# Linear attention with a gated MLP: the query sums as unsplit fp32 products in two column halves of the array, and GpSimd in program order around them

## The chip, the cores and the metric

The kernel runs on one core of one Trainium2 chip. TensorE (PE in the profile) multiplies matrices, with its weight loads recorded separately (PEld); VectorE (DVE), ScalarE (ACT) and GpSimd (POOL) do elementwise work; SyncE (SP) and GpSimd issue DMA transfers. A fp32r operand is a 32-bit number that TensorE reads in one pass at reduced precision; a number split into two fp32r parts, high and low, keeps nearly all of fp32's digits. The metric is the device time in microseconds of one execution, the median of several runs.

## The reference

One input x of 2048 tokens by 576 features goes through two layers, and a gate per token mixes them. The attention layer has 32 heads of 18 features, and each head's feature map phi has 36 (two softmaxes).

```python
pq = einsum("bhsd,hdf->bhsf", q, w_phi)
phi_q = concatenate([softmax(pq), softmax(-pq)])      # the same for phi_k
kv = einsum("bhsf,bhsd->bhfd", phi_k, v)
z = einsum("bhsf->bhf", phi_k)
num = einsum("bhqf,bhfd->bhqd", phi_q, kv)
den = einsum("bhqf,bhf->bhq", phi_q, z)[..., None] + 1e-6
a = (num / den) @ wo                                  # heads side by side
h = (x @ W_gate) * (x @ W_gate > 0) * (x @ W_up)
b = h @ W_down                                        # 4608 hidden features
return g * a + (1 - g) * b                            # g = sigmoid(x . gate_w)
```

## The kernel before, in words

**Stages.** The 2048 tokens are 16 tiles of 128, or four blocks of 512, worked through in the order 3, 0, 1, 2 (`BLOCKS`); "block 0" to "block 3" below count in that order. From 0 to 262 us the kernel makes projections, softmaxes, and the key sums kv and z over all tokens. From 262 to 300 us it makes the query sums (num and den) of blocks 0 and 1. From there to 365 us it divides, multiplies by wo (`project_out`, tiles pw, lines 738 to 759) and makes the sums of blocks 2 and 3 between. From 365 to 400 us the last output projection overlaps the start of the MLP, and from 400 us the MLP runs alone.

**Query sums.** Heads lie in groups: three heads are 54 output columns and 108 rows of phi (`QK`); eleven such groups hold 32 heads (`NQ`; the last has two). `sums` (L537) makes the sums of two groups, that is six heads, in one PSUM tile, as 108 columns of num and six of den (`QM` = 114). Each group takes three fp32r products of 512 columns: weights high by queries high, high by low, low by high. Six pairs of groups are taken in the order 4, 5, 3, 2, 1, 0 (`ORDER`). The weights kvm are a block-diagonal arrangement of kv and z, split into kvh (L527) and kvl (L531). The queries of block 0 are turned in place from PSUM (`turn`, ptr) into their parts phh and phl (L150, L151). Those of the other blocks go to memory (eT) and come back tile by tile as er (`fetch`, L425), and ACT (L435) and DVE (L439) split them.

**What follows a sum.** `sums_out` (L546) copies the PSUM tile to R, or to the separate tile og for pairs 4 and 5 (L552, ACT). SP sends the den rows to a tile dn (L554). GpSimd issues the fills (L556, L559, L560): they move num rows of og into free rows of R, so that five full tiles of 128 rows come out. `invert` (L695) takes the reciprocal of dn, multiplies it by the gate and splits it into rdh and rdl (L706, L708). `divide` (L711) spreads them over the rows with a product (pd) and multiplies R by it (L717); the result is split into oh and ol for the product with wo. `rows_out` (L762) copies the finished rows and stores them to att, by GpSimd for three of the blocks.

**What sets the order.** A scheduler orders the instructions of each engine by their dependences and by tile buffers, apart from those named in `in_order` (L53): there the engine keeps the order of the program. Before, that holds for TensorE only. Each engine then carries out its own list strictly in order, and so does each queue of DMA issues. A tile whose buffer is still read by an earlier user makes its writer wait. `scale` (L210) multiplies the softmax numerators e by the reciprocals of their sums; the last ones, on GpSimd, stand in this stretch.

**The hand-over.** `load_w` (L830) loads raw MLP weights (wr, 768 KB each) that ACT and DVE split into wb and ws (`unit`, L887). On SP they stand where the scheduler finds their buffer free.

Of the kernel before, what the change touches and what calls it, by code (L numbers as in the profile page):

```python
# [35 lines left out]
QM = G + 2 * QH  # L36
# [46 lines left out]
def gated_mix_kernel(  # L83
# [281 lines left out]
    def turn(t, b, ps=None):  # L365
# [52 lines left out]
    def operands(tb):  # L418
        PH[tb] = [[ph.tile([QK, len(n), TB], F32R, name=f"ph{a}{n.start}") for a in "hl"] for n in QN]

    ER = {}
# [5 lines left out]
    def part(tb, i, p):  # L427
        if tb not in PH:
            operands(tb)
        return *(a[:, :, i * P:(i + 1) * P] for a in PH[tb][p]), ER[4 * tb + i][:, QN[p].start:QN[p].stop]  # L430

    def prepare_high(tb, i, p):

        h, l, r = part(tb, i, p)
        nc.scalar.activation(h, r, AF.Copy)  # L435

    def prepare_low(tb, i, p):
        h, l, r = part(tb, i, p)
        tt(out=l, in0=r, in1=h.bitcast(F32), op=SUB)  # L439
# [16 lines left out]
    for t in range(2, NT - 2):  # L456
# [10 lines left out]
        if t == 12:  # L467
# [6 lines left out]
            ph = RS.enter_context(tc.tile_pool(name="ph", bufs=1, **R_))  # L474
# [35 lines left out]
    def kv_blocks(q):  # L510

        n, ps = min(4, NQ - 4 * q), PKV[q]
        for p in range(2):
# [7 lines left out]
            else:  # L521
                tt(out=kvm[:, gs_, p * QG:(p + 1) * QG], in0=ps[:, p:n:2, 1 + p * QG:1 + (p + 1) * QG],
                   in1=mask[:, None, :].to_broadcast([QK, ng, QG]), op=MULT)
            nc.vector.scalar_tensor_tensor(
                out=kvm[:, gs_, G + 3 * p:G + 3 * p + 3], in0=ps[:, p:n:2, 0:1].to_broadcast([QK, ng, 3]),
                scalar=eps, in1=hm[:, None, :].to_broadcast([QK, ng, 3]), op0=ADD, op1=MULT)
        nc.scalar.activation(kvh[:, 4 * q:4 * q + n, :QM], kvm[:, 4 * q:4 * q + n], AF.Copy)  # L527

    def kv_low(q):
        n = min(4, NQ - 4 * q)  # L530
        tt(out=kvl[:, 4 * q:4 * q + n, :QM], in0=kvm[:, 4 * q:4 * q + n],  # L531
           in1=kvh[:, 4 * q:4 * q + n, :QM].bitcast(F32), op=SUB)

# [3 lines left out]
    def sums(tb, i, ps):  # L537

        PS[tb, i] = ps = ps[:QM]
        parts, pairs = PH[BLOCKS[tb]], []  # L540
        for g in range(2 * i, min(2 * i + 2, NQ)):
            (h, l), o = parts[g // 4], g % 4
            pairs += [(kvh[:, g, :QM], h[:, o]), (kvh[:, g, :QM], l[:, o]), (kvl[:, g, :QM], h[:, o])]
        accumulate(ps, pairs)

    def sums_out(tb, i):  # L546
# [4 lines left out]
        og = OG[i] = R[:QM, i] if i < 4 else rb.tile([P, TB], F32, name="og")[:QM]  # L551
        nc.scalar.activation(og, PS.pop((tb, i)), AF.Copy)  # L552
        d0, dl = (G, HG) if i < NJ - 1 else (G + 1, 2)
        nc.sync.dma_start(dn[4 * HG * i:4 * (HG * i + dl)], og[d0:d0 + dl])  # L554
        if i < 4:
            nc.gpsimd.dma_start(R[G:, i], OG[4][20 * i:20 * i + 20])  # L556
# [34 lines left out]
    with in_order(tc, nc, nc.tensor):  # L591
# [10 lines left out]
        er = RS.enter_context(tc.tile_pool(name="er", bufs=4, **R_))  # L602
# [3 lines left out]
        kvm = kb.tile([QK, NQ * QM + 26], F32, name="kvm")[:, :NQ * QM].rearrange("p (g c) -> p g c", g=NQ)  # L606
        kvh = kb.tile([QK, NQ, P], F32R, name="kvh")
        kvl = kb.tile([QK, NQ, P], F32R, name="kvl")
# [4 lines left out]
        for i in range(4):  # L613
            fetch(i)
# [13 lines left out]
        kv_low(2)  # L628
# [3 lines left out]
        kv_low(1)  # L632
        turn(t, 0)
        kv_low(0)
# [4 lines left out]
        for n, i in enumerate(ORDER):  # L639
# [22 lines left out]
        for i in range(4):  # L662
            prepare_high(b1, i, 0)
            prepare_low(b1, i, 0)
# [230 lines left out]
    def prepare_tile(n, i):  # L895
        tb = BLOCKS[n]
        for p in (2, 1, 0):
            prepare_high(tb, i, p)
            prepare_low(tb, i, p)

# [20 lines left out]
    with in_order(tc, nc, nc.tensor):  # L921
# [14 lines left out]
        for i in range(4):  # L936
            fetch(4 * BLOCKS[2] + i)
        inv = invert(1)
        for k in range(5):
# [8 lines left out]
            if k < 3:  # L948
                prepare_tile(2, k)
            if k >= 3:  # L950
                divide(1, k - 3)
                project_out(0, k - 2, (1,))
                if k == 3:
                    prepare_tile(2, 3)
# [19 lines left out]
        for i in range(4):  # L974
            fetch(4 * BLOCKS[3] + i)
# [8 lines left out]
        for k in range(5):  # L984
            project_out(1, k)
            if k < 4:
                prepare_tile(3, k)
# [584 lines left out]
def _layout(A_x, A_wqkv, A_w_phi, A_wo, B_W_gate, B_W_up, B_W_down, gate_w):  # L1572
# [17 lines left out]
    wo_rows = [r for k in range(4) for r in (*range(G * k, G * k + G), *range(4 * G + 20 * k, 4 * G + 20 * k + 20))]  # L1590
    wo_rows += [*range(512, D)] * 2
# [40 lines left out]
```

## Time and profile before

| what | us |
|---|---|
| median of 3 runs | 1642.44 (1641.4 to 1642.8) |
| profiled execution: span | 1636.5 |
| TensorE busy in it | 1604.4 (98%) |
| TensorE busy, 262 to 300 us | 30.74 of 38, mean clock 0.91 |
| TensorE busy, 300 to 365 us | 65.00 of 65 |
| TensorE busy, 365 to 400 us | 30.05 of 35 |

The runs' times lie some 6 us above the span, which counts from the first to the last recorded instruction. A group row reads: line, engine, operation, output <- input, shapes, count | busy us, mean ns | idle time of the engine just before, and what ended it. A timeline row reads: start, duration, engine, line, operation, output <- input, and in brackets the idle time before it. Records of one matmul overlap those of the next, so their spacing, not their length, tells what one costs.

### The profile page before, as it was taken

Reading aid. Unit: us, or ns where it says so; the run is one execution under the profiler, and the core shown is the slowest. Engines: PE = TensorE matmul, PEld = TensorE weight load, DVE = VectorE, ACT = ScalarE, POOL = GpSimd, SP = SyncE. Lnnn points to the kernel's source line nnn. Section 1 sums busy time; section 2 is a strip of 40 time slices with the busy share of each in tenths; the row PEclk is TensorE's granted clock in tenths of the full one; section 3 lists DMA queues with packets and bytes.
Section 4 is the critical chain, followed back from the end, with each engine's and each line's share of the span. In section 5 each row is a group of like instructions: output and inputs, shape, how many; then the busy total and the mean of one; then the engine's idle time right before and its main releaser. Section 6 shows DMA issues by size and latency. Waiting matters only on the chain.

```text
span 1636.5 us, 20150 instructions
## 1 busy us (share of the span) xinstructions
PE 1604.4 (98%) x7732; PEld 1348.2 (82%) x7732; DVE 1232.1 (75%) x1908; ACT 581.4 (36%) x962; POOL 182.3 (11%) x266
## 2 busy tenths in 40 slices
PE   9999998998999999999999999999999999999998
PEld 8898997787788888888888887778888888888887
DVE  4988777758777777877777777667777677777777
ACT  4344335645333333332333334222322323223231
POOL 0128212220000000000000002111111111111110
PEclk9999999999999999999999999999999999999999
DMA  8243115565865656555645533553444434344442
GB/s 266 94 145 153 58 46 189 188 203 205 305 234 196 232 217 234 213 209 213 223 189 190 193 143 129 190 205 140 160 150 145 180 127 183 128 172 154 148 163 73
DMA packets 64860, 285.80 MB, mean 175 GB/s; under 512 B 7290, under 2 KB 16890, under 8 KB 55804
## 3 DMA queue, kind: packets, MB, share of 16 engines
q1 hardware_dynamic: 61932, 278.22, 46.9%
q0 software_dynamic: 2256, 5.25, 1.0%
q8 instruction: 61, 1.00, 0.2%
q10 hardware_dynamic: 576, 1.05, 0.2%
q14 instruction: 35, 0.29, 0.1%
HBM read 172.99 MB, written 109.54 MB: 173 GB/s over the span
## 4 chain that ended last, share of the span: by engine, by line
PE 87%; DVE 4%; DMA 4%; issue 2%; ACT 2%; POOL 1%; SPq 0%; ACTq 0%; DVEq 0%; POOLq 0%
PE cx L1132 26%; PE ca L1132 13%; PE pd L1172 12%; PE pd L1195 10%; PE cy L1132 7%; PE pq L177 3%; PE pv L177 2%; PE pk L177 2%; PE pm L1172 2%; PE pw L759 2%; PE pm L1195 2%; PE kv L411 2%; DMA wdr<-wd 1%; PE ptr L371 1%; PE pv L239 1%
## 5 line engine op out<-in xcount | busy, mean ns | idle before, releaser
L1239 ACT ACTIVATE hh<-g 128x512 fp32r<-128x512 f32 x195 | 120.0, 624 | 454.5 <-DVE g L1289 285.2
L1210 DVE TENSOR_TENSOR ac<-pd,ac 128x512 f32<-128x512 f32 x238 | 164.0, 689 | 146.4 <-PE pd L1195 146.3
L1132 PE MATMUL cx<-xo,ws 128*128 128x512 f32 x1008 | 252.7, 390 | 4.9 <-ACT g L1293 4.9
L1132 PE MATMUL ca<-xo,ws 128*128 128x512 f32 x1008 | 252.0, 389 | 0.6 <-DMA ws<-wsd 0.6
L1132 PE MATMUL cx<-xo,wb 128*128 128x512 f32 x1008 | 249.4, 390 | 3.0 <-DMA wb<-wbd 1.7
L1132 PEld LDWEIGHTS cx<-xo,ws 128*128 128x128 f32 x1008 | 189.1, 188 | 45.4 <-ACT g L1293 6.2
L1132 PEld LDWEIGHTS cx<-xo,wb 128*128 128x128 f32 x1008 | 188.0, 188 | 44.7 <-DVE u L1414 2.2
L1132 PEld LDWEIGHTS ca<-xo,ws 128*128 128x128 f32 x1008 | 189.1, 188 | 40.3 <-issue 1.0
L1172 PE MATMUL pd<-hh,wd 128*128 128x512 f32 x576 | 200.7, 389 | 0.0
L1195 PE MATMUL pd<-hh,wd 128*128 128x512 f32 x476 | 185.2, 389 | 0.0
L1178 DVE TENSOR_TENSOR ac<-pd,ac 128x512 f32<-128x512 f32 x144 | 99.0, 688 | 105.8 <-PE pd L1172 102.3
L1244 DVE TENSOR_TENSOR hl<-g,hh 128x512 fp32r<-128x512 f32 x195 | 136.1, 698 | 1.9 <-ACT hh L1239 0.2
L1293 ACT ACTIVATE g<-cx 128x512 f32<-128x512 f32 x144 | 85.0, 590 | 127.4 <-PE cx L1132 127.3
L1132 PE MATMUL cy<-xo,wb 128*128 128x512 f32 x504 | 127.2, 392 | 0.0
L1172 PEld LDWEIGHTS pd<-hh,wd 128*128 128x128 f32 x576 | 108.1, 188 | 22.5
L1095 ACT ACTIVATE wd<-wdr 128x384 fp32r<-128x384 f32 (+1 forms) x106 | 62.3, 606 | 155.7 <-DMA wdr<-wd 155.7
L1172 PE MATMUL pd<-hl,wd 128*128 128x512 f32 x288 | 112.1, 389 | 1.0 <-ACT xo L821 1.0
L1132 PEld LDWEIGHTS cy<-xo,wb 128*128 128x128 f32 x504 | 95.6, 190 | 20.1
L1195 PEld LDWEIGHTS pd<-hh,wd 128*128 128x128 f32 x476 | 89.4, 188 | 18.6
L1195 PE MATMUL pd<-hl,wd 128*128 128x512 f32 x238 | 92.6, 389 | 0.0
L805 POOL TENSOR_TENSOR xo<-xr,xo 32x512 fp32r<-32x512 f32 x5 | 8.2, 1651 | 634.6 <-DVE xo L805 627.3
L1098 DVE TENSOR_TENSOR wd<-wdr,wd 128x384 fp32r<-128x384 f32 (+1 forms) x106 | 69.7, 672 | 6.4 <-ACT wd L1095 6.4
(241 smaller groups left out, 2732.1 us busy)
## 6 DMA issues: line engine op xcount, KB each, us to landing
wsd<-ws SPq DMA_DIRECT2D x34, 1280.0 KB
ws<-wsd SPq DMA_DIRECT2D x34, 1280.0 KB
wbd<-wb SPq DMA_DIRECT2D x34, 960.0 KB
wb<-wbd SPq DMA_DIRECT2D x34, 960.0 KB
wr<-wgu SPq DMA_DIRECT2D x36, 768.0 KB
wdr<-wd SPq DMA_DIRECT2D x36, 576.0 KB
eT<-et SPq DMA_DIRECT2D x12, 594.0 KB
er<-eT SPq DMA_DIRECT2D x12, 594.0 KB
```

The source lines that it names most:

```text
L177: nc.tensor.matmul(ps, w, m, start=i == 0, stop=i == len(pairs) - 1)
L411: nc.tensor.matmul(kv[j // 2][:vn + 1, j % 2, :gn], v[:, j * GS:j * GS + vn + 1], flat(e)[:, c0:c0 + gn], start=False, stop=t == NT - 1, s ...
L1095: nc.scalar.activation(o[:, 0], a, AF.Copy)
L1098: tt(out=o[:, 1], in0=a, in1=o[:, 0].bitcast(F32), op=SUB)
L1132: nc.tensor.matmul(ps, w, v, start=first and m == 0, stop=m == len(pairs) - 1, skip_group_check=True)
L1172: nc.tensor.matmul(ps, w, v, start=k == 0 and (i < 2 or first), stop=k == len(mms) - 1 and (i < 2 or last), skip_group_check=True)
L1178: tt(out=a, in0=ps, in1=a, op=ADD)
L1195: mm = lambda ps, w, v, a, z: nc.tensor.matmul(ps, w, v, start=a, stop=z, skip_group_check=True)
L1210: tt(out=a, in0=ps, in1=a, op=ADD)
L1239: nc.scalar.activation(h, src, AF.Copy)
L1244: tt(out=l, in0=src, in1=h.bitcast(F32), op=SUB)
L1293: nc.scalar.activation(a, ps, AF.Copy)
```

## The change

Each group of three heads becomes one fp32 product of unsplit weights (kvm, 64 columns: 54 of num, three of den, the rest zero) and unsplit queries. The even group of a pair goes to the PSUM partitions 0 to 63 and the odd one to 64 to 127, which are the two halves of the array's columns. The splits of kvm and of the queries go, with the parts phh, phl, kvh, kvl and the tiles er; the queries of blocks 1 to 3 are loaded straight into place, with two buffers, and with an earlier place in the program. The copies take 128 rows, each pair's den rows are two DMAs instead of one, and a block's fills are 14 instead of 8, with fewer rows each. The rows of wo and spread are permuted on the host to fit. GpSimd joins TensorE in program order in the stretch that ends with block 1's turning.

```diff
-QM = G + 2 * QH
+QM = 64
...
         if t >= FIRST:
-            h, l = (a[:, :, t % 4 * P:(t % 4 + 1) * P] for a in PH[t // 4][b])
-            split(h, l, ps[:, :len(gg)])
+            nc.scalar.activation(PH[t // 4][:, t % 4, gg.start:gg.stop], ps[:, :len(gg)], AF.Copy)
...
-    def fetch(t):
-        ER[t] = er.tile([QK, NQ, P], F32, name="er")
-        nc.sync.dma_start(ER[t].rearrange("p g t -> p (g t)"), eT[t * QK:(t + 1) * QK])
+        PH[tb] = ph.tile([QK, 4, NQ, P], F32, name="ph")
+
+    def fetch(tb):
+        operands(tb)
+        for i in range(4):
+            t = 4 * tb + i
+            nc.sync.dma_start(PH[tb][:, i].rearrange("p g t -> p (g t)"), eT[t * QK:(t + 1) * QK])
...
-            ph = RS.enter_context(tc.tile_pool(name="ph", bufs=1, **R_))
+            ph = RS.enter_context(tc.tile_pool(name="ph", bufs=2, **R_))
...
-        PS[tb, i] = ps = ps[:QM]
-        parts, pairs = PH[BLOCKS[tb]], []
+        PS[tb, i] = ps
         for g in range(2 * i, min(2 * i + 2, NQ)):
-            (h, l), o = parts[g // 4], g % 4
-            pairs += [(kvh[:, g, :QM], h[:, o]), (kvh[:, g, :QM], l[:, o]), (kvl[:, g, :QM], h[:, o])]
-        accumulate(ps, pairs)
+            nc.tensor.matmul(ps[g % 2 * 64:g % 2 * 64 + QM], kvm[:, g], PH[BLOCKS[tb]][:, :, g], start=True, stop=True)
...
-        d0, dl = (G, HG) if i < NJ - 1 else (G + 1, 2)
-        nc.sync.dma_start(dn[4 * HG * i:4 * (HG * i + dl)], og[d0:d0 + dl])
+        if i < NJ - 1:
+            for p in range(2):
+                nc.sync.dma_start(dn[4 * (HG * i + QH * p):4 * (HG * i + QH * p + QH)], og[64 * p + QG:64 * p + QG + QH])
+        else:
+            nc.sync.dma_start(dn[4 * HG * i:], og[QG + 1:QG + QH])
         if i < 4:
-            nc.gpsimd.dma_start(R[G:, i], OG[4][20 * i:20 * i + 20])
+            for p in range(2):
+                nc.gpsimd.dma_start(R[64 * p + QG:64 * p + 64, i], OG[4][64 * p + 10 * i:64 * p + 10 * i + 10])
         elif i == 5:
             for r in (0, 64):
-                nc.gpsimd.dma_start(R[r:r + 28, 4], OG[4][80:G])
+                for p in range(2):
+                    nc.gpsimd.dma_start(R[r + 14 * p:r + 14 * p + 14, 4], OG[4][64 * p + 40:64 * p + QG])
                 nc.gpsimd.dma_start(R[r + 28:r + 64, 4], OG[5][DH:QG])
...
-    with in_order(tc, nc, nc.tensor):
+    with in_order(tc, nc, nc.tensor, nc.gpsimd):
...
-        for i in range(4):
-            fetch(i)
+        fetch(BLOCKS[1])
...
-            if n in (3, 5):
-                for i in range(4):
-                    prepare_high(b1, i, 2 - n // 4)
-                    prepare_low(b1, i, 2 - n // 4)
         PH.pop(b0)
+        fetch(BLOCKS[2])
```

GpSimd's list, from the last but one scaling in this stretch on, before (e is a tile of softmax numerators; the rows in L556 to L560 are the fills of block 0):

```order
L211 TENSOR_TENSOR e<-e,r 128x32x18 [waits DVE_49,Activation_49]
L559 DMA R<-og 28x512 [waits Activation_49,Pool_49]
L560 DMA R<-og 36x512 [waits Activation_49]
L559 DMA R<-og 28x512
L560 DMA R<-og 36x512
L556 DMA R<-og 20x512 [waits DMAHW0_49,Activation_49]
L211 TENSOR_TENSOR e<-e,r 128x32x18 [waits DVE_49,Activation_49]
L556 DMA R<-og 20x512 [waits DMAHW2_49,Activation_49]
```

and after (L541 and L542 are the fills of R's fifth tile, L537 those of the other four):

```order
L211 TENSOR_TENSOR e<-e,r 128x32x18 [waits DVE_49,PE_49,Activation_49] x2
L541 DMA R<-og 14x512 [waits DMAHW5_49,DMAHW7_49,DMAHW4_49,DMAHW3_49]
L541 DMA R<-og 14x512
L542 DMA R<-og 36x512 [waits Activation_49]
L541 DMA R<-og 14x512 x2
L542 DMA R<-og 36x512
L537 DMA R<-og 10x512 [waits DMAHW2_49,Activation_49]
L537 DMA R<-og 10x512 [waits DMAHW3_49]
```

Both scalings now stand ahead of all fills; before, the last one stood behind a fill that waits for a transfer.

ACT's list around block 1's first copies, before (phh is the high part of block 1's and block 2's queries, rdh that of block 0's reciprocals):

```order
L435 ACTIVATE phh_2866<-er 108x4x128 x2
L552 ACTIVATE og<-po 114x512 [waits DMASW3_49,DMASW1_49,DMAHW7_49,PE_49,Activation_49]
L552 ACTIVATE og<-po 114x512 [waits DMASW5_49,DMASW6_49,DMASW4_49,DMASW7_49,DMASW2_49,DMAHW5_49,DMASW0_49,PE_49]
L706 ACTIVATE rdh<-rd 128x512 [waits DMAHW4_49,DMAHW3_49,DVE_49]
L552 ACTIVATE R<-po 114x512 [waits PE_49] x2
L435 ACTIVATE phh_3127<-er 108x3x128 [waits DMAHW0_49,Activation_49]
```

and after:

```order
L529 ACTIVATE og<-po 128x512 [waits DMASW5_49,DMASW2_49,DMAHW1_49,PE_49,Activation_49]
L529 ACTIVATE og<-po 64x512 [waits DMASW5_49,DMASW4_49,DMASW6_49,DMASW3_49,DMASW7_49,DMASW2_49,DMAHW0_49,DMASW1_49,DMAHW7_49,DMASW0_49,PE_49]
L675 ACTIVATE rdh<-rd 128x512 [waits DMAHW5_49,DMAHW0_49,DVE_49]
L529 ACTIVATE R<-po 128x512 [waits PE_49] x2
L688 ACTIVATE oh<-R 128x512 [waits DMAHW7_49,DVE_49,Activation_49]
```

The split steps are gone from ACT's list; the second copy of og, which waits on all eight of GpSimd's DMA semaphores (DMASW), still stands ahead of rdh.

SP's list where the first raw MLP weights stand, before (behind the last loads of x for the MLP):

```order
L815 DMA xr<-xt 128x512 [waits DMAHW1_49]
L810 DMA xo<-xt 128x1024 [waits DMAHW2_49]
L833 DMA wr<-wgu 128x1536 [waits DMASW5_49,DMASW4_49,DMASW6_49,DMASW3_49,DMASW7_49,DMASW2_49,DMAHW3_49,DMASW1_49,DMASW0_49]
L833 DMA wr<-wgu 128x1536 [waits DMAHW4_49,Pool_49]
```

and after (behind the queries of block 1, ahead of block 0's denominators):

```order
L424 DMA ph<-eT 108x1408 [waits DMAHW2_49]
L802 DMA wr<-wgu 128x1536 [waits DMAHW3_49,PE_49]
L802 DMA wr<-wgu 128x1536 [waits DMAHW4_49,PE_49,Pool_49]
L651 DMA spread<-sprd 128x640 [waits DMAHW5_49,PE_49]
L652 DMA wo_h<-wohd 128x3200 [waits DMAHW6_49,DVE_49,PE_49]
L532 DMA dn<-og 12x1x128 [waits DMAHW7_49,Activation_49]
```

The two weight loads moved from behind the sums of the last block to ahead of those of the first.

More of the change, by code (lines that the diff above doesn't have):

```diff
@@ L521, in kv_blocks @@
             else:
-                tt(out=kvm[:, gs_, p * QG:(p + 1) * QG], in0=ps[:, p:n:2, 1 + p * QG:1 + (p + 1) * QG],
+                tt(out=kvm[:, gs_, :QG], in0=ps[:, p:n:2, 1 + p * QG:1 + (p + 1) * QG],
                    in1=mask[:, None, :].to_broadcast([QK, ng, QG]), op=MULT)
             nc.vector.scalar_tensor_tensor(
-                out=kvm[:, gs_, G + 3 * p:G + 3 * p + 3], in0=ps[:, p:n:2, 0:1].to_broadcast([QK, ng, 3]),
+                out=kvm[:, gs_, QG:QG + QH], in0=ps[:, p:n:2, 0:1].to_broadcast([QK, ng, 3]),
                 scalar=eps, in1=hm[:, None, :].to_broadcast([QK, ng, 3]), op0=ADD, op1=MULT)
[L527 to L532, printed above, removed]
     DN, RW, OG, PS = {}, {}, {}, {}
@@ L605, in gated_mix_kernel @@
         mask, hm, eps = table[:, :QG], table[:, QG:QG + 3], table[:, QG + 3:]
-        kvm = kb.tile([QK, NQ * QM + 26], F32, name="kvm")[:, :NQ * QM].rearrange("p (g c) -> p g c", g=NQ)
-        kvh = kb.tile([QK, NQ, P], F32R, name="kvh")
-        kvl = kb.tile([QK, NQ, P], F32R, name="kvl")
+        kvm = kb.tile([QK, NQ, QM], F32, name="kvm")
         cmask = kb.tile([P, P, 1], F32, name="cmask")[:, :4]
@@ L661, in gated_mix_kernel @@
         turn(FIRST - 1, 2, two[:, 1])
-        for i in range(4):
-            prepare_high(b1, i, 0)
-            prepare_low(b1, i, 0)
         A.close()
@@ L935, in gated_mix_kernel @@
         divide(0, 4)
-        for i in range(4):
-            fetch(4 * BLOCKS[2] + i)
+        fetch(BLOCKS[3])
         inv = invert(1)
@@ L973, in gated_mix_kernel @@
         block(2)
-        for i in range(4):
-            fetch(4 * BLOCKS[3] + i)
         def in_place(i):
```

37 lines of the change are left out of this document (6 added, 31 removed).

## The prediction

> **What bounds the kernel now.** I read the page first, then the busy time by stage, then the chain of waits inside the stage that the diff touches.
>
> ```profile
> span 1636.5 us, 20150 instructions
> PE 1604.4 (98%) x7732; PEld 1348.2 (82%) x7732; DVE 1232.1 (75%) x1908; ACT 581.4 (36%) x962; POOL 182.3 (11%) x266
> PE 87%; DVE 4%; DMA 4%; issue 2%; ACT 2%; POOL 1%; SPq 0%; ACTq 0%; DVEq 0%; POOLq 0%
> ```
>
> TensorE is busy for 98% of the span, so there are two ways to gain: shorter matmul work, or less of the 32 us in which TensorE idles. The stages (start, length, PE busy first, then the granted clock and the DMA share before the last number) tell where each lies:
>
> ```profile
> core 0: us, PE busy (x) PEld busy (x) DVE busy (x) ACT busy (x) POOL busy (x), PEclk, DMA share, GB/s
> 262.00:300.00 38.00, 30.74 (x151) 23.14 (x150) 27.06 (x60) 25.15 (x47) 9.66 (x16) 0.91 0.73 234
> 300.00:365.00 65.00, 65.00 (x289) 52.52 (x289) 44.70 (x70) 37.01 (x66) 14.38 (x29) 1.00 0.59 190
> 365.00:400.00 35.00, 30.05 (x123) 23.73 (x123) 28.55 (x39) 21.00 (x31) 2.77 (x5) 0.95 0.48 161
> ```
>
> The changed code works from 262 to 365. From 300 to 365 TensorE never idles: there only matmul time counts, and work taken off ACT, DVE or the queues is worth nothing. From 262 to 300 it idles 7.3 us and runs at a clock of 0.91: there waits count. From 365 to 400 it idles 5 us. What follows is untouched. The chain of waits (start, length, what) in the second and fourth stage:
>
> ```profile
> 273.58 6.12 DMA dn<-R
> ...
> 280.23 0.51 POOL R L556
> 280.75 2.01 POOL e L211
> 282.81 1.97 PE ptr L371 x8
> ...
> 287.29 7.84 DMA er<-eT
> 295.22 0.53 ACT phh L435
> ...
> 299.52 9.99 PE pw L759 x44
> ...
> 318.17 2.76 PE po L177 x12
> ...
> 355.35 9.63 issue
> 365.00 4.09 DMA att<-o
> ```
>
> Three waits stand there. The last scaling on GpSimd (e L211) sits behind a fill (R L556) that waits for a landing (dn). Block 2's raw queries (er) land 7.84 us after their issue and hold up ACT, in program order, in front of the copies of block 1. An output store (att) holds up a buffer in the hand-over. The first output product (pw) starts at 299.5; from there to 365 the matmuls set the time.
>
> **Matmul time: the sums.** Before, a block takes 33 products of 512 columns, 132 in all; 12 take 2.76 us, so one takes 0.230 us and a block 7.6 us. After, a block takes 11 products in fp32. No fp32 product of 512 columns stands in this trace; the nearest are the key sums (kv, 216 columns), which are recorded twice per product, so twelve records are six products:
>
> ```profile
> 219.58 2.13 PE kv L411 x12
> L411 PE MATMUL kv<-e,vt x10: 346/346/346, 219.4 to 221.1; 128*109 128x216 f32 x10
> 221.33 0.14 PEld L411 LDWEIGHTS kv<-e,vt 128*37 128x37 f32 x2 [0.28 <-issue]
> 221.64 0.19 PEld L177 LDWEIGHTS pk<-wk_h,xh 128*128 128x128 f32 x1 [0.16 <-issue]
> ```
>
> Five products of 216 columns are ten records, whose starts lie (221.1 − 219.4)/9 = 0.19 us apart. The whole chain piece has 2 x (5 x 216 + 108) = 2376 columns in 2.13 us; less the 0.12 us of a break described next, that is 0.846 ns a column, 0.433 us for 512, and 0.87 us for an fp32 product. Against three split products (0.69 us) that is dearer, by 1.25. Only if the two groups, which go to separate column halves, run side by side is the new form cheaper.
>
> The break is the second price. The product with 37 columns of weights goes to a smaller tile of the array, and the loads stop for 0.28 us before it and 0.16 us behind it, 0.44 together. Matmuls still in the array run on in part of that time, so I take three quarters, 0.32 us a visit; at the full 0.44 the six visits of blocks 2 and 3 would cost 0.7 us more. Every run of sums between other matmuls becomes such a visit: four in block 0, three in each other block. The Trainium skill has this as a rule that speaks against the change (TensorEngine Tiling (Array Packing), Key Properties): changing the tiling mode, not just the tile, drains TensorE. The trace agrees, with the 0.28 and 0.16 just shown; the page gives no figure, so by it the sum below stays at −3.6 with the row's 0.32.
>
> Side by side, a visit of n products takes n + 1 records of 0.433 (each has two, and the halves overlap except at the ends). Blocks 2 and 3 have visits of 3, 4 and 4: 14 x 0.433 + 3 x 0.32 = 7.0 us against 7.6, 0.6 less each, on the path: −1.2 us. One after another it is 22 x 0.433 + 0.96 = 10.5, 2.9 more each: +5.7 us. No row shows which holds, so −1.2 and +5.7 are both ends of the range. I take the first, because two halves share no columns, though the in-order stream of weights and records speaks less clearly for it. The Trainium skill (TensorE: Matmul & The Clock Gate, Part 3) reports that three tiles in separate columns, of 32 columns each, went 2.38 times as fast as one after another; no run here shows it yet, and by it the sum would be the first, −3.6 against +4.7.
>
> Blocks 0 and 1 (8.2 and 7.4 us side by side against 7.6) lie in the stage with idle TensorE, and are part of the next term.
>
> **262 to 300: waits removed, and what is late next.** First the windows of this stage's middle, then single instructions in order of time (in brackets idle time and its releaser), then the fills' median landing and the two split steps from the groups of 262 to 400.
>
> ```profile
> 280.00:285.00 5.00, 1.95 (x8) 1.54 (x8) 1.73 (x3) 1.36 (x4) 3.49 (x4) 0.70 0.90 303
> 285.00:290.00 5.00, 4.55 (x15) 3.59 (x16) 3.81 (x7) 3.83 (x8) 0.64 (x2) 0.61 0.56 160
> 282.81 1.95 PE L371 MATMUL ptr<-ident,e 128*108 128x128 f32 x8 [3.06 <-POOL e L211]
> 285.98 0.78 PE L177 MATMUL po<-phh,kvh 108*114 108x512 f32 x1
> 288.62 0.95 DVE L698 RECIPROCAL dn<-dn 128x128 f32<-128x128 f32 x1
> 288.98 1.29 ACT L552 ACTIVATE og<-po 114x512 f32<-114x512 f32 x2 [1.08 <-issue]
> 290.66 0.63 ACT L706 ACTIVATE rdh<-rd 128x512 fp32r<-128x512 f32 x1 [0.40 <-DVE rd L702]
> 292.23 0.40 PE L177 MATMUL pd<-rdh,spread 128*128 128x512 f32 x1
> 295.90 0.39 PE L177 MATMUL po<-phh,kvl 108*114 108x512 f32 x1
> R<-og POOLq DMA_DIRECT2D x4, 72.0 KB, 5.7
> R<-og POOLq DMA_DIRECT2D x7, 40.0 KB, 4.1
> L439 DVE TENSOR_TENSOR phl<-er,phh 108x512 fp32r<-108x512 f32 (+1 forms) x36 | 21.8, 637 | 6.6 <-ACT phh L435 6.4
> L435 ACT ACTIVATE phh<-er 108x512 fp32r<-108x512 f32 (+1 forms) x36 | 19.2, 591 | 3.6 <-DMA er<-eT 3.6
> ```
>
> What goes: the scaling e L211 no longer waits behind the fill. The matmuls that it releases start near 278 instead of 282.81, and block 1's sums near 281 instead of 285.98. The er wait goes with its ACT and DVE steps, so the sums are not held up between the divisions. If nothing else were late, the division would follow block 0's denominators: the last of them issued near 279, landed near 282 (estimates from 6.12 us for an earlier one under heavier traffic, and the fills' 4 us). From the reciprocal to the first division passed 3.6 us (288.62 to 292.23), from there to the first output product 7.3 (299.52). That gives 292.9, or 6.6 us sooner.
>
> What is late next: on ACT the copy of the two-head group's sums (og, 64x512) stands ahead of rdh, and its buffer is the one from which block 0's fills read, so it waits until all fourteen have landed. Before there were eight, the copies went at 288.98 and rdh at 290.66. GpSimd has six more issues at 0.51 us, 3.1 us, which fit between the landings; the last two can go near 282.5. Landing took 4.1 to 5.7 us, and now the 2.4 MB of block 2's queries are issued on SP just ahead of them. I take 6 us: 288.5, og until 289.1, rdh and its low part until 290.6, first division near 290.8. The 7.3 us behind it held the er wait, but the copies, divisions and splits that alternate there stay; I take 7.3 again. First output product: 298.1 against 299.5, so −1.4 us. TensorE would idle some 5 us between block 1's sums and the first division. Above, 3.06 us of idling were followed by windows at a clock of 0.70 and 0.61, so part of the 7.3 may run at that clock. Ends: −6.6 (the fills land no later than the denominators), and +1.5 (they land 2.9 us later than I take, after 9 us, a little beyond the 7.84 of the er load).
>
> **365 to 372.** The store att holds the buffer for the last addition of block 2's rows, and TensorE stands 2.03 us:
>
> ```profile
> 355.00:360.00 5.00, 5.00 (x24) 4.14 (x23) 3.53 (x6) 2.01 (x2) 0.35 (x1) 1.00 1.01 302
> 354.76 1.10 SPq L833 DMA_DIRECT2D wr<-wgu x2
> att<-o POOLq DMA_DIRECT2D x12, 256.0 KB, 3.3
> 371.76 0.47 PE L759 MATMUL pw<-oh,wo_h 128*128 128x512 f32 x1 [2.03 <-DVE o L771]
> ```
>
> The two weight loads wr (1.5 MB, 5 us at the 302 GB/s of that window) leave this traffic, because in the new order on SP they go out a hundred us earlier, behind block 1's queries. The store took 4.09 us and 3.3 at the median, so I take 1 us off: −1.0. Ends: 0 (other loads fill the same time) and −2.0 (the whole gap).
>
> **What costs nothing, and under what cover.** The 36 splits each on ACT and DVE (19.2 and 21.8 us), beyond those on the path above: from 300 to 365 TensorE is busy throughout, and the queries now come straight into place. The wr loads on SP: their issue takes 1.10 us, soon after block 1's queries (near 256, if nothing holds their buffer), ahead of the denominators, whose first landing in the chain is awaited from 273.58; their 5 us of traffic is over by then. Without that cover the denominators land up to 5 us late, which is case c below. Five more denominator issues a block on SP, at 0.7 to 0.8 us: alone they cost up to 3.8 us, but the division of the next blocks comes some 10 us behind them. The rows of 128 instead of 114 in copies: the same 512 columns, as the rows above show (1.29 us for two copies of 114 rows, 0.63 for rdh with 128). The lower output weights (wo_l, 1280 KB) now go behind the queries and the last turned tile: 4.3 MB from 279, 14 us at 302 GB/s, so until 293; they are used from the third output step, after 304.
>
> **Sum.** −1.4 − 1.2 − 1.0 = −3.6 us. The profiled span is 1636.5; the runs' median is 1642.4, 5.9 above it, which I leave as it is. So about 1639.0 us, span 1633.
>
> **Rivals.**
> a) The forecast. Its own range is 1636.5 to 1641.5, from the landing's spread of about 2 us either way. 42%.
> b) The fills land with the denominators, and TensorE never idles long enough for the lower clock: −6.6 − 1.2 − 1.0, 1633.6 us. For it: GpSimd's queue is free earlier, fills of 10 rows are half as large as those of 20. Against: 2.4 MB in front. 17%.
> c) The fills or the denominators come late (wr and block 2's queries in front), the first output product 1.5 later: +1.5 − 1.2 − 1.0, 1641.7 us. 10%.
> d) The two halves run one after another. Blocks 2 and 3 then cost +5.7; block 1's sums end near 287, which makes the first division no later than the fills do, but the sums of both blocks stretch by 2.9 us each, so I let the first term fall to 0; with −1.0 for the hand-over +4.7, 1647.1 us. For it: each fp32 product is two records with weight loads of their own, in one instruction stream, and any load that waits for the other half's matmul ends the overlap. Between full overlap (−3.6) and none (+4.7) lie 8.3 us, so it decides where less than 1 − 3.6/8.3 = 57% of the overlap comes about. 27%.
> e) Something that no row names, of either sign. 4%.
>
> 0.2% is 3.3 us, about what a measurement of this kernel can tell from no change: faster is below 1639.2, slower above 1645.7. Of a, I put 25 in 100 below 1639.2 and 17 above; b is all faster, c same, d slower, e two each way: faster 44, same 27, slower 29. The range 1633 to 1649 reaches from b to d with a part of each one's spread left out.
>
> **What the profile after would show.** Products of the sums (64 columns, partition halves) whose starts pair up: a visit of four products in about 2.2 us shows the overlap, 3.5 us its absence. The scaling e L211 near 275, without a fill ahead of it. On ACT the 64x512 copy og released by a DMA, near 288.5; a first output product at 298. No er landing in the chain. The wr issue near 256, and a TensorE gap near 370 of about 1 us. The prediction is wrong if the halves serialize, if TensorE idles in 300 to 365 (queries of block 2 or 3, or a fill, come late), or if a change of the tile size costs much more than 0.32 us: at 1 us a visit, the six visits of blocks 2 and 3 alone would cost 4 us more.

## The result

The changed kernel took 1644.36 us at the median of 11 runs (1640.40 to 1646.33), against 1641.40 for the kernel before in the same job (1637.77 to 1642.84): a ratio of 1.002, with a 95% interval of 1.0012 to 1.0029. It is slower by some 3 us, where the prediction's likeliest case was 3.6 us faster. The time lies inside the stated range, but on the wrong side of the kernel before.

The profiled execution of the changed kernel is its slowest run (1646.33 us, 1.7 above its span), and the one shown of the kernel before is one of its faster kind. So the spans, 1644.6 and 1636.5, lie further apart than the medians. The windows from 40 to 80 us, ahead of everything that the change touches, show 3 us of that; the rows are before, the kernel before profiled once more, and the changed kernel (PE busy first, the granted clock third from the end), the last with the windows of the changed stages:

```profile
40.00:80.00 40.00, 36.36 (x251) 34.20 (x251) 37.77 (x57) 14.06 (x23) 7.52 (x7) 0.96 0.24 83
```
```profile
40.00:80.00 40.00, 36.52 (x227) 34.08 (x227) 34.42 (x50) 12.52 (x21) 6.31 (x5) 0.87 0.23 75
```
```profile
40.00:80.00 40.00, 36.26 (x225) 33.92 (x224) 34.34 (x50) 12.28 (x20) 6.30 (x5) 0.87 0.22 75
262.00:300.00 38.00, 22.47 (x128) 13.04 (x127) 12.61 (x35) 14.69 (x28) 12.71 (x22) 0.87 0.64 215
300.00:365.00 65.00, 64.88 (x261) 42.39 (x262) 32.69 (x49) 28.19 (x47) 24.24 (x46) 0.94 0.50 158
365.00:400.00 35.00, 31.24 (x129) 24.45 (x127) 28.14 (x38) 21.06 (x31) 2.75 (x5) 0.95 0.43 144
290.00:300.00 10.00, 0.79 (x1) 0.29 (x1) 0.69 (x1) 2.07 (x4) 2.06 (x4) 0.52 0.89 295
300.00:310.00 10.00, 9.94 (x26) 4.90 (x27) 5.07 (x9) 3.72 (x6) 3.60 (x7) 0.63 0.27 74
```

An unchanged kernel shows either clock there (0.96 or 0.87), so this stretch is chance and is taken out: below, times are counted from the last query projection (pq), whose first record starts at 266.70 in the changed kernel, 3.07 us later than before. The row before, from TensorE's timeline:

```profile
263.63 0.38 PE L177 MATMUL pq<-wq_h,xh 128*128 128x288 f32 x1
```

The stage from 262 to 300 lost 8 us of busy TensorE, and between 290 and 300 it stood almost still. The timeline of TensorE in the changed kernel names two waits:

```profile
266.70 0.38 PE L177 MATMUL pq<-wq_h,xh 128*128 128x288 f32 x1
281.61 3.65 PE L520 MATMUL po<-ph,kvm 108*64 108x512 f32 x14
297.36 0.79 PE L177 MATMUL pd<-rdh,spread 128*128 128x512 f32 x1 [12.10 <-ACT rdh L675]
300.06 0.80 PE L177 MATMUL pd<-rdl,spread 128*128 128x512 f32 x1 [1.90 <-DVE rdl L677]
308.00 0.40 PE L728 MATMUL pw<-oh,wo_h 128*128 128x512 f32 x1
326.73 1.94 PE L520 MATMUL po<-ph,kvm 108*64 108x512 f32 x8
328.60 0.50 PE L177 MATMUL pd<-rdh,spread 128*128 128x512 f32 x1
328.94 0.40 PE L177 MATMUL pd<-rdl,spread 128*128 128x512 f32 x1
378.01 0.47 PE L728 MATMUL pw<-oh,wo_h 128*128 128x512 f32 x1 [2.21 <-DVE o L740]
391.74 0.62 PE L1086 MATMUL cx<-xo,wb 128*128 128x512 f32 x2
```

| stretch | before | after | difference |
|---|---|---|---|
| last query projection to first output product (pw) | 35.7 | 41.3 | +5.6 |
| from there to the last output block's first product | 72.4 | 70.0 | −2.4 |
| from there to the first MLP product (cx) | 12.1 | 13.7 | +1.6 |
| MLP to the end | 1252.6 | 1252.9 | +0.2 |

The sum is +5.0 us in these two executions, and about +3 in the medians. The fourth stretch is unchanged; the third is the half clock after a gap of 2.21 us (see the end). The work of ACT, GpSimd, DVE and SP around the first stretch, from their timelines:

```profile
276.43 1.17 POOL L211 TENSOR_TENSOR e<-e,r 128x576 f32<-128x576 f32 x1 [12.24 <-PE ptr L371]
283.98 1.85 SPq L424 DMA_DIRECT2D ph<-eT  x4
285.93 0.75 SPq L386 DMA_DIRECT2D eT<-et  x1
286.73 0.42 SPq L653 DMA_DIRECT2D wo_l<-wold  x1
286.60 1.07 POOL L537 DMA_DIRECT2D R<-og  x2 [2.74 <-DMA dn<-R]
296.20 0.59 ACT L529 ACTIVATE og<-po 64x512 f32<-64x512 f32 x1 [12.82 <-DMA R<-og]
296.69 0.62 ACT L675 ACTIVATE rdh<-rd 128x512 fp32r<-128x512 f32 x1
299.31 0.69 DVE L677 TENSOR_TENSOR rdl<-rd,rdh 128x512 fp32r<-128x512 f32 x1 [10.45 <-DMA eT<-et]
```

Block 2's queries (four loads, 2.4 MB), the last turned tile's store (eT) and the lower output weights (wo_l) were issued between 284 and 287 us. Block 0's last two fills were issued at 286.6 to 287.7, when the last of its denominators had landed; they held up the copy og until 296.2, and rdh stands behind og in ACT's order. The store eT landed only at 299.2 (13.26 us in the chain of waits); by the releaser, rdl waited for it. The program has no such dependence, so a place in SBUF that the turned tile had held is the likely reason, which no run tests. So two small steps stood behind the same bulk, and TensorE idled 12.10 and 1.90 us and then ran at a clock of 0.52 and 0.63.

The sums themselves are quicker than before. The visit of four products starts at 326.73, and the second product of the division behind it at 328.94, 2.21 us later. In the kernel before, the two products of a division start 0.23 us apart; with that, the visit takes 1.98 us, against 2.76 for the twelve split products of before.

### The profile page after: what moved, and what is told of

Its sections match the earlier page's. It is cut to its first block, busy times and chain, and to the rows that moved or that the text cites. A ratio compares the mean times of both kernels' runs of the same rounds, so it can differ in the third digit from the quotient of the medians.

```text
span 1644.6 us, 20003 instructions
## 1 busy us (share of the span) xinstructions
PE 1604.2 (98%) x7688; PEld 1334.7 (81%) x7688; DVE 1205.0 (73%) x1857; ACT 561.9 (34%) x923; POOL 193.4 (12%) x290
## 3 DMA queue, kind: packets, MB, share of 16 engines
q0 software_dynamic: 3024, 5.25, 1.0%
## 4 chain that ended last, share of the span: by engine, by line
PE 87%; DMA 4%; issue 3%; DVE 3%; ACT 2%; POOL 1%; SPq 0%; POOLq 0%; ACTq 0%; DVEq 0%
PE cx L1086 27%; PE ca L1086 13%; PE pd L1126 12%; PE pd L1149 10%; PE cy L1086 7%; PE pq L177 3%; PE pk L177 3%; PE pv L177 2%; PE pm L1126 2%; PE pm L1149 2%; PE kv L410 2%; PE pw L728 1%; DMA wdr<-wd 1%; PE ptr L371 1%; PE pv L239 1%
```

## The experiments

All ratios are to the kernel before, run in the same job. In the table, A is the time from the last query projection to the first output product, and B from there to the first MLP product, both read from one profile each. A profiled execution lies up to 7.2 us from the median of its version (by tile: 1637.78 against 1645.02), so A and B explain a ratio only roughly.

| version | ratio (95% interval) | A | B |
|---|---|---|---|
| before | 1 | 35.7 (again: 34.9) | 84.5 (85.2) |
| changed | 1.0020 (1.0012 to 1.0029) | 41.3 | 83.7 |
| late fetch | 1.0026 (1.0015 to 1.0037) | 32.9 | 91.3 |
| four og buffers | 1.0048 (1.0035 to 1.0061) | 42.2 | 86.2 |
| GpSimd free | 1.0019 (1.0011 to 1.0028) | 41.7 | 82.0 |
| one tile | 1.0069 (1.0057 to 1.0082) | 43.3 | 87.8 |
| both loads behind | 1.0017 (1.0006 to 1.0029) | 32.7 | 88.8 |
| by tile | 1.0025 (1.0011 to 1.0038) | 33.0 | 88.1 |
| by tile, block 3 late | 1.0013 (1.0002 to 1.0024) | 33.1 | 91.4 |
| block 2 behind, block 3 late | 1.0000 (0.9992 to 1.0009) | 33.0 | 85.3 |
| the same with one denominator DMA | 0.9960 (0.9947 to 0.9972) | 33.4 | 80.8 |
| changed with one denominator DMA | 1.0014 (1.0004 to 1.0024) | 42.8 | 82.2 |

**Late fetch.** The load of block 2's queries moves into the sums of block 1.

```diff
         PH.pop(b0)
-        fetch(BLOCKS[2])
...
             if n == 2:
                 whole(inv)
+                fetch(BLOCKS[2])
```

> The changed kernel with the load of block 2's queries moved from behind block 0's sums to behind the third of block 1's sums; on ACT the two-head copy og then stands behind rdh. Theory 1 (traffic): in the changed kernel 4.3 MB of loads issued at 284 to 287 us delayed block 0's last fills and the store of the last turned tile, on which og and rdl wait. Then here rdh goes near 289, rdl near 290, TensorE idles 5 us instead of 12, the first output product starts near 298 to 299 instead of 308, and the ratio to before is about 0.997 (changed kernel 1.002). Theory 2 (GpSimd's program order made the fills late): the first fills still go near 277.5, so the gain is at most the 1 to 2 us of the ACT order, ratio 1.001.

A fell by 8.4 us: the first output product went at 296.76, or 299.6 on the changed kernel's time. The scheduler made a second change, as the expectation says: rdh now stands ahead of the copy og. ACT's timeline in this version:

```profile
286.10 0.63 ACT L674 ACTIVATE rdh<-rd 128x512 fp32r<-128x512 f32 x1 [5.57 <-DVE rd L670]
290.82 0.58 ACT L529 ACTIVATE og<-po 64x512 f32<-64x512 f32 x1
```

The last fill of block 0 landed 5.99 us after its issue instead of 8.64, and og still came 4.7 us after rdh. In the old order rdh would have gone at about 291 (an estimate: the last fill landed at 290.3), so more of the gain at this gate is the order's than the load's. At the other gate no order changed: rdl no longer waited for the store eT and went right behind rdh, at 286.76.

The total gained nothing, because B rose by 7.6. The chain of waits shows the same wait one block later, with block 1's denominators behind the moved load and then its fills behind block 3's:

```profile
284.35 5.99 DMA R<-og
...
294.64 10.37 DMA dn<-R
...
308.62 8.63 DMA R<-og
```

Theory 2 falls, since GpSimd's order was the same. Theory 1 holds for rdl, and for the fills in part. The expected ratio was a miss: the bulk was moved, not removed.

**Four og buffers.** One number changes, the buffers of og.

```diff
-        og = OG[i] = (R[:, i] if i < 4 else rb.tile([P, TB], F32, name="og"))[:n]
+        og = OG[i] = (R[:, i] if i < 4 else rb.tile([P, TB], F32, name="og", bufs=4))[:n]
```

> The changed kernel with four buffers for og instead of two, so that og of block 1 waits for no fill. Theory 1 with two gates (fills before og, and the store of the last turned tile before rdl): rdh near 289, but rdl still near 299, first output product near 306 instead of 308, ratio 1.001. If the fills were the only gate: rdl near 290, first output product near 298, ratio 0.996 to 0.997.

From the timelines of ACT, DVE and SP in this version:

```profile
288.82 0.63 ACT L675 ACTIVATE rdh<-rd 128x512 fp32r<-128x512 f32 x1 [4.66 <-DVE rd L671]
301.30 0.69 DVE L677 TENSOR_TENSOR rdl<-rd,rdh 128x512 fp32r<-128x512 f32 x1 [12.51 <-DMA eT<-et]
292.41 17.15 SPq L532 DMA_DIRECT2D dn<-R  x8
309.66 2.27 SPq L424 DMA_DIRECT2D ph<-eT  x4
```

With og's wait gone, rdh went at 288.8 as expected and rdl still waited for the store, until 301.3: there are two gates, and taking one away is worth nothing in A. This version and the late fetch differ little up to rdh (22.1 and 22.2 us behind the start of A); with the load in front A is 42.2, without it 32.9. That is the clearest evidence that the load is the cause. That the kernel became slower than the changed one (1.0048) was not expected. Block 1's denominators filled SP's list for 17 us, each waiting for the copies behind the late division, and block 3's load stood behind them, 1.6 us later than in the changed kernel (308.05); how much of the loss that makes was not separated.

**GpSimd free.** The scheduler orders GpSimd again.

```diff
-    with in_order(tc, nc, nc.tensor, nc.gpsimd):
+    with in_order(tc, nc, nc.tensor):
```

> The changed kernel with GpSimd left to the scheduler (the in-order list names TensorE alone, as before). Theory 2: the fills of R's fifth tile go near 272 again and the last ones earlier too, first output product 3 us or more sooner, ratio 1.000. Theory 1: the last fills still meet the same loads, so og and rdl are as late as in the changed kernel, and the last scaling may fall behind a fill again; ratio 1.002 to 1.003.

The first fills went at 273.2 instead of 277.5, and the last two at 286.2 instead of 286.6, since they wait for the denominators; the copy og still waited, 10.61 us. The ratio is that of the changed kernel. In these versions GpSimd's program order is neither the loss nor a gain.

**One tile.** The two products of a pair accumulate in one full tile, with zeros in the other half of the weights (the lines that fill kvm so are left out).

```diff
-        nc.tensor.matmul(ps[g % 2 * 64:g % 2 * 64 + QM], kvm[:, g], ...)
+        one = i == NJ - 1
+        nc.tensor.matmul(ps[:QM] if one else ps, kvm[:, g, :QM] if one else kvm[:, g], ...,
+                         start=g == 2 * i, stop=one or g == 2 * i + 1)
```

> The changed kernel without the column halves: weights of 128 columns with zeros in the other group's half, the two products of a pair accumulate, in the full tile. If the halves run side by side in the changed kernel (a visit of four products took 1.87 us there, two after two of 0.87), a block here takes 22 records of 0.433, 9.5 us, against some 6.2: +3.3 in each of blocks 2 and 3, ratio near 1.006. If side by side gains nothing, the time is that of the changed kernel less the changes of tile size, ratio 1.000 to 1.002.

Three rows of TensorE's timeline in this version, a visit of four products and the division that follows it:

```profile
329.70 3.60 PE L521 MATMUL po<-ph,kvm 108*128 108x512 f32 x8
332.73 0.80 PE L177 MATMUL pd<-rdh,spread 128*128 128x512 f32 x1
333.36 0.40 PE L177 MATMUL pd<-rdl,spread 128*128 128x512 f32 x1
```

The division's first product is recorded as starting 0.03 us after the start of the eighth record, so its start is no end of the visit. Measured as above, to the division's second product, it is 3.67 us against 2.21 in the halves: 3.43 us for four products (eight records, 0.43 apart) against 1.98. The time rises by some 8 us against the changed kernel. The two column halves do run side by side; this version without them costs 0.7% against the kernel before.

**Both loads behind, and by tile.** First both query loads stand behind block 1's denominators; then block 2's is cut into tiles between them.

```diff
         PH.pop(b0)
-        fetch(BLOCKS[2])
...
         divide(0, 4)
+        fetch(BLOCKS[2])
         fetch(BLOCKS[3])
```

> The changed kernel with the query loads of blocks 2 and 3 both behind the last of block 1's denominators. Moving block 2's load between them (the late fetch) freed block 0's small transfers but put block 1's behind 2.4 MB instead: a denominator took 10.4 us and a fill 8.6 us there. If small transfers queued behind the query loads are the cause, here neither block's denominators stand behind one: first output product as early as in the late fetch, block 1's reciprocal near 299 instead of 306, no idle TensorE near 305 to 320, ratio 0.997 to 0.998. Rival: the queries come too late for block 2's sums (needed near 316), or the last fills of block 1 (issued after the loads) do: TensorE waits there instead, ratio 1.000 or above.

```diff
             if n == 2:
                 whole(inv)
+            if n >= 2:
+                fetch(BLOCKS[2], [n - 2])
```

> The late fetch with block 2's load cut into its four tiles of 594 KB, one behind each of the last four of block 1's sums, as the kernel before spread them. If what counts is how much stands ahead of a small transfer, each denominator is some 2 us late instead of 10, block 1's reciprocal near 300, ratio 0.998 to 0.999. If only the bytes in flight count, as late as with the whole load: ratio 1.002 to 1.003.

Both keep A at 33 us and block 1's divisions come earlier than in the late fetch. In the first, the reciprocal of block 1 went at 298.42, as expected, but TensorE idled near 316 all the same. The store att of block 0's rows (issued at 311.8 behind eight query loads and two loads of x) held up the buffer b, and ACT's copies behind it, as the timelines of SP, GpSimd, ACT and TensorE in that version show:

```profile
296.18 3.96 SPq L424 DMA_DIRECT2D ph<-eT  x8
300.89 2.56 SPq L748 DMA_DIRECT2D xr<-xt  x2
311.77 1.13 POOL L740 DMA_DIRECT2D att<-o  x2 [12.79 <-ACT o L735]
318.11 0.59 ACT L738 ACTIVATE b<-pw 64x512 f32<-64x512 f32 x1 [4.14 <-DMA att<-o]
319.89 1.12 PE L520 MATMUL po<-ph,kvm 108*64 108x512 f32 x2 [3.49 <-ACT R L529]
```

The expected 0.997 was missed by both. In the one by tile the reciprocal went at 303.8 and the fill behind it made DVE wait 5.25 us.

**The kernel before, again.**

> The kernel before, profiled once more. Its runs fall near 1638 or near 1642, and the profile shown of it is of the first kind, with a half clock of some 3.5 us at 45 to 50; the changed kernel's profile has some 3 us more of it at 45 to 60, a stage which the change does not touch. If that is chance, this profile may show either, and nothing between 300 and 400 differs.

This settled the early stretch, as shown in the result. From 300 to 365 us TensorE idled 0.91 us in it, against none in the first profile, so single executions differ by about 1 us there too.

**Block 3's queries late.** In the last two versions block 3's load moves to where the kernel before had it.

```diff
-        fetch(BLOCKS[3])
...
         block(2)
+        fetch(BLOCKS[3])
```

> Block 2's queries by tile between block 1's denominators, and block 3's queries (needed near 341) behind block 2's sums, where the kernel before had them, instead of right behind block 1. If the stores att and the fills of block 1 were late in the earlier trials because 2.4 MB of block 3's queries stood in front of them, the idle time of TensorE between 305 and 325 goes, and the time falls by some 2 to 4 us against the version by tile: ratio 0.998 to 1.000. If not, it stays at 1.002.

> Block 2's queries behind the last of block 1's denominators, block 3's behind block 2's sums: no small transfer of blocks 0 and 1 and no store att stands behind more than 2.4 MB of queries. If small transfers behind query loads are all that the changed kernel loses, TensorE no longer idles 3.5 us near 316 as with both loads together, and the ratio is 0.997 to 0.998; a ratio of 1.001 or more says that something else is lost.

The scheduler carried the edit out only in part: three of the four tiles of block 3 were still issued at 304 to 308 in the version by tile, two of four in the other. By tile, TensorE still idled 3.83 us near 327, and the ratio stayed above 1. The other, with less in front, came level with the kernel before. There the first division was now held by block 0's denominators (through the reciprocal, rdh and the copy behind it), of which SP's list showed the last two issued from 282.49, 2.8 us behind the copy at 279.68 from which they read (timelines of ACT, SP, DVE and TensorE in that version):

```profile
279.68 0.60 ACT L529 ACTIVATE R<-kv 128x512 f32<-128x512 f32 x1 [0.88 <-PE kv L520]
278.05 3.84 SPq L532 DMA_DIRECT2D dn<-R  x5
282.49 2.08 SPq L532 DMA_DIRECT2D dn<-R  x2
287.59 0.95 DVE L666 RECIPROCAL dn<-dn 128x128 f32<-128x128 f32 x1 [8.37 <-DMA dn<-R]
290.87 0.79 PE L177 MATMUL pd<-rdh,spread 128*128 128x512 f32 x1 [4.87 <-ACT R L529]
```

**One denominator DMA.** The denominators' columns move to the inner edges of the halves, so that the six rows of a pair are neighbours. This was done on the last version and on the changed kernel.

```diff
-            for p in range(2):
-                nc.sync.dma_start(dn[4 * (HG * i + QH * p):4 * (HG * i + QH * p + QH)], og[64 * p + QG:64 * p + QG + QH])
+        d0, dl = (QM - QH, HG) if i < NJ - 1 else (QM - 2, 2)
+        nc.sync.dma_start(dn[4 * HG * i:4 * (HG * i + dl)], og[d0:d0 + dl])
...
-            for p in range(2):
-                nc.gpsimd.dma_start(R[64 * p + QG:64 * p + 64, i], OG[4][64 * p + 10 * i:64 * p + 10 * i + 10])
+            nc.gpsimd.dma_start(R[54:67, i], OG[4][13 * i:13 * i + 13])
+            nc.gpsimd.dma_start(R[121:, i], OG[4][67 + 7 * i:74 + 7 * i])
```

> The version with block 2's queries behind block 1's denominators and block 3's behind block 2's sums, and besides the denominators' columns put at the inner edges of the two halves (61 to 63 and 64 to 66), so that a pair's six rows leave by one DMA again; fills stay two per pair. If SP's list of eleven issues of 0.77 us held back block 0's last denominators (issued 2.9 us behind their copy there, landed at 287.3, TensorE idle 4.9 us before the first division), they land 2 to 3 us sooner, the idle time falls to 2 to 3 us, and the ratio is 0.997 to 0.999. If not SP but the transfer sets their landing, as before: 1.000.

> The changed kernel with one DMA for a pair's six denominators, the query loads left where they were in the program. If the doubled denominators are what made the changed kernel slow, ratio near 0.998 to 1.000 and the first output product 5 us or more sooner; if the query loads in front of the fills and of the last turned tile's store are, they stay in front, and the ratio is 1.001 to 1.002.

On the late version it gave 1634.64 us, a ratio of 0.996 (0.9947 to 0.9972), the only version faster than both kernels. On the changed kernel it gave 1.0014, as the theory of the loads in front had it: the copy og still waited 9.68 us and rdl until 299.7. In the fast version block 0's reciprocal is early, and TensorE idles in pieces of 1.09, 1.76, 2.12 and 1.26 us. Three rows of its timelines, and the window of the stage that gained:

```profile
276.31 0.76 SPq L531 DMA_DIRECT2D dn<-R  x1
281.78 0.95 DVE L663 RECIPROCAL dn<-dn 128x128 f32<-128x128 f32 x1 [6.57 <-DMA dn<-R]
285.05 0.50 PE L177 MATMUL pd<-rdh,spread 128*128 128x512 f32 x1 [1.76 <-ACT R L529]
300.00:365.00 65.00, 64.20 (x276) 44.85 (x274) 34.48 (x51) 30.26 (x51) 23.81 (x45) 1.00 0.57 199
```

A did not fall further, so the reason that the expectation gave, an earlier first division, did not bring the gain; it lies in B, 80.8 against 85.3. The version before it idled 2.53 us ahead of a visit of block 2's sums (at 324.51) and had a clock of 0.83 from 320 to 330; here neither is found, and TensorE is busy for 64.20 of the 65 us. The scheduler also spread block 2's loads otherwise in this version (tiles issued from 279.37 to 296.20) and issued the lower output weights some 11 us earlier, so the gain is that of the shorter list of issues together with the placing that followed from it. The two were not separated.

## Why the prediction was wrong, point by point

- **The step that failed** is the first term of the sum, "What is late next": the landing of block 0's last fills. The prediction saw that the copy og stands ahead of rdh and waits for the fills, and that block 2's queries go out just ahead of them. It gave the landing 6 us, with 9 as the bound. In the prediction's time, 3.07 us earlier than the changed kernel's, the last fill was issued at 284.1 instead of 282.5, since it waited for the denominators. It landed 8.6 us later and not 6, still below the bound, and og was released at 293.1 instead of 288.5, so the first division went at 294.3 instead of 290.8.
- The prediction had the number that tells this. For the lower output weights it worked out 4.3 MB of traffic from 279, "so until 293", but it did not set the landing of the fills or of the turned tile's store by it. The fills' median landing in the trace of before came from traffic in which SP's loads were spread, four tiles one by one. That the load is the cause shows best in the four og buffers against the late fetch, 42.2 against 32.9 in A.
- **What was missing** is the second gate: rdl, which waited for the last turned tile's store. It cost another 1.90 us of idling in the changed kernel, and the four og buffers showed that it alone suffices to keep the division at 302. In the trace that the prediction read, this store ended no wait; in the second profile of the kernel before it ended one of 1.20 us.
- **Behind the first division** the prediction took 7.3 us to the first output product and said that part of it may run at a lower clock. It took 10.6 (297.36 to 308.00), with the 1.90 us at rdl. In the late fetch, where rdl did not wait, it took 9.5 (287.27 to 296.76) at a clock of 0.62 from 290 to 300. So some 2 us were missing here even without the loads in front.
- So the first term came out at +5.6 instead of −1.4, and beyond its upper end of +1.5. Case c had this mechanism, at a quarter of its size and a chance of 10%. That the range holds the measured time is luck: its upper part was there for case d, which the runs refute.
- **The sums** were forecast in the right direction and too small: −1.2 for blocks 2 and 3. By the rows a block takes 6.2 us instead of 7.6, so −2.8; the stretch that holds both measured −2.4. The halves run side by side, and closer than by n + 1 records: a visit lasts as long as the larger count of one half. With both changes of tile, four products take 2.07 us, where the model gave 2.5, and three 2.06, where it gave 2.05. The price of 0.32 us a visit was about right: 2.07 is 0.35 more than four records of 0.43, of which 0.09 lies at the entry and 0.10 at the exit (spacings of 0.32 and 0.34 us instead of 0.23). The term that was mis-sized is the additional record. Case d, the halves one after another, is refuted by these rows and the one-tile version. The 8.2 and 7.4 us for blocks 0 and 1 do not follow from the prediction's own rule, which gives 7.8 and 7.0; they enter no sum.
- The Trainium skill's two rules (TensorEngine Tiling (Array Packing), Key Properties; TensorE: Matmul & The Clock Gate, Part 3) agree with these rows: the change of mode costs time at both ends, 0.09 and 0.10 us, and separate column tiles run at once, here 1.98 us for four products in halves of 64 columns against 3.43 in one tile.
- **The hand-over**, −1.0, did not come: the wr loads went out at 258.5 as foreseen, the store att took 3.43 us instead of 4.09, and TensorE stood 2.21 us instead of 2.03. Over all versions and both profiles of the kernel before this gap lies between 1.16 and 3.64 us, so no gain by the wr loads can be told, and the −1.0 was not tested by itself.
- **Costed at nothing**: the doubled denominator issues, "the division of the next blocks comes some 10 us behind them". In the changed kernel the last two fills waited 2.74 us for the last of these transfers, so part of their late issue is due to it. Joining the transfers alone changed little there (1.0014 against 1.0020, with intervals that overlap). Where the loads were out of the way, block 0's denominators on SP became the gate; joining them came with the only gain, though A did not fall by it.
- The time itself was set against the median of three runs, 5.9 us above the span; but the profiled execution was none of these three (its span and 1.7 us give 1638.2), and a run lies 1.7 us above its own span, not some 6. The forecast change of −3.6 us is not affected.

## What to carry to other kernels

When a change replaces small loads that a few buffers spread out by one large load issued as soon as its buffer is free, look at what small transfer is issued next, and who waits for it: here the waits for 40 KB of fills and a 594 KB store cost more than the matmuls gained. If a prediction has worked out how long the traffic lasts, it should hold every transfer issued in that time against it. A load needs to be early only by as much as its user needs it. Moving it behind the last small transfer of one chain helped that chain, and moved the wait to the next one. A change of matmul form can be right and still lose; the version with the same products and the transfers in better order was 0.4% faster than the kernel before.

## What the runs showed of the hardware that was not expected

- The length of one wait does not tell whether the clock falls. An idle TensorE of 2.03 us (before, at 371.76) left the clock at 1.00, and one of 2.21 us (changed, at 378.01) was followed by a window with a clock of 0.50, in which products lie 0.43 us apart instead of 0.23. But a wait of 1.81 us in the version by tile was followed by half the clock too, and one of 2.69 us in the second profile of the kernel before (at 393.48) by none. The third stretch of the table became 1.6 us longer by the half clock. The rows of the changed kernel, then of the version by tile:

```profile
378.00:380.00 2.00, 1.99 (x7) 1.62 (x8) 1.95 (x3) 0.00 (x0) 0.56 (x1) 0.78 0.29 66
380.00:382.00 2.00, 2.00 (x6) 1.52 (x6) 1.86 (x5) 0.00 (x0) 0.00 (x0) 0.50 0.00 0
```
```profile
370.54 0.47 PE L728 MATMUL pw<-oh,wo_h 128*128 128x512 f32 x1 [1.81 <-DVE o L740]
372.00:374.00 2.00, 2.00 (x7) 1.52 (x6) 1.88 (x5) 0.00 (x0) 0.00 (x0) 0.50 0.16 35
```

- The half clock between 40 and 80 us lasts about 3 us in one execution of a kernel and about 10 in another (0.96 and 0.87 over 40 us, in the two profiles of the kernel before). The last query projection came 3.64 us later in the second (267.27 against 263.63), which is as much as the whole change moved.
- The scaling e L211 took 2.00 us before, beside split steps on DVE, and 1.17 in the changed kernel, with the same 128x576 elements; the earlier scalings of this form took 1.16 to 1.17 in both kernels (210 to 264 us), and the one in this place 1.79 in the second profile of the kernel before. The cause was not tested.
